# Soft-capped attention and a maxout layer on one core: three buffers for q and k, with their loads and crossbar transposes moved forward in the order

## The chip, the cores and the metric

The kernel runs on one core of a Trainium2 chip. Its time is the device time of one execution in microseconds (us); lower is better. Several runs were timed, and one more execution was taken by the hardware profiler, which is where all instruction times below come from.

The engines by the profile's names: PE is the matrix engine (PEld its weight loads), DVE the vector engine, ACT the scalar engine with its function tables, POOL the GpSimd engine, which here issues loads, and SP the sync engine, which here issues crossbar transposes and stores. A "q" behind an engine's name is its instruction queue.

## What is computed

Attention over 8 batches of 12 heads, 448 rows and 64 columns, with a soft cap of 30 on the scores; then a layer that takes the larger of two products, and an output product. The reference, cut:

```python
scores = scale * np.matmul(q, k.transpose(0, 1, 3, 2))     # (8, 12, 448, 64) each
scores = cap * np.tanh(scores / cap)
scores = scores - np.max(scores, axis=-1, keepdims=True)
attn = np.exp(scores)
attn = attn / (np.sum(attn, axis=-1, keepdims=True) + 1e-09)
attn_out = np.matmul(attn, v)
...
x = attn_out.transpose(0, 2, 1, 3).reshape(B * S, H * D)   # 3584 x 768
h1 = x @ w1                                                # 768 x 1024
h2 = x @ w2
g = np.maximum(h1, h2)
return g @ w_out                                           # 1024 x 768
```

## The kernel before

**Tiling.** Two heads of one batch make a pair, two pairs a quad. There are 48 pairs and 24 quads, three quads to a batch. The maxout layer is rewritten: max(h1, h2) = h2 + max(h1 - h2, 0), so the kernel prepares w1 - w2 (`wd_sb`) and w2 times w_out (`wm_sb`) once, and the layer needs a product with `wd_sb` (stage 1), a relu (L619), and products with `wm_sb` and `wo_sb` (stage 2).

**The order.** Nothing is left to a scheduler. The string `ORDER` (from L9) lists some 2300 steps, and the loop at L699 runs them one after the other; each step emits a few instructions, and every engine and queue executes its own in this order. Where an instruction needs a buffer or data of another engine, it waits there, and what is behind it on the same engine waits too. A step's place in `ORDER` relative to steps on other engines has no force of its own: it matters only through the waits, and through what stands before it on its own engine.

**The steps that matter here.**

- `lk i x`, `lq i 0` (`load`, L318): POOL issues loads of k and q of pair i into `kqs`, turning f32 into bf16 on the way. From pair 10 on (`NX = 10`) k comes in two parts and q in one (L329), so a quad has four k loads and two q loads. A quad's rows lie in `kqs[t % KB]`, with `KB = 2` buffers (L267, L270).
- `cr t` (`cross`, L443): from quad 5 on SP issues one crossbar transpose (a DMA) that turns the whole quad from `kqs` into a `qkT` buffer, of which there are `QB = 2` (L415, L445). In the first five quads PE does this turning with an identity matrix (L430), and DVE copies the result (L435).
- `S i j` (`scores`, L473): PE multiplies k and q of pair i from `qkT` (L478), for row block j of three. `L t` (L485, L491) does the left-over 64 rows of both pairs of quad t. A score tile is one of two `s` buffers in PSUM.
- `T`, `TL`, `E`, `EL`: ACT's tanh (L483, L495) and exponential (L499, L502).
- `A`, `B`, `Y`, `Y1` to `Y3`: sums of the exponentials and their inverses, on DVE and PE.
- `lv t p` (`load_v`, L331): POOL issues the four loads of the values of quad t, with `VB = 2` buffers, so that they wait for the values product of quad t-2.
- `V t u` (`values`, L553): PE multiplies the exponentials with the values (L561, L565), and `N` (L574) scales the result on DVE into `xT`. `V t` comes after the scores of pair 2t + 2, so some one and a half quads after the scores of quad t begin.
- `M x y n` (`moe`, L677): n matmuls each of groups x and y of the layer (L598), put between the attention's steps to fill PE. `H` is a hand-over between the two halves of a group, `ev` copies a finished group out of PSUM (L619 for stage 1, L652 for stage 2 into one of four `osb` buffers).
- `st b t` (`store`, L623): SP issues the two stores of an output tile (L634, or L629 and L630).

So in the steady state four chains meet: POOL's loads fill `kqs`, SP turns `kqs` into `qkT`, PE reads `qkT`, and the buffers go back: loads of quad t wait until the transpose of quad t - KB has landed, and the transpose of quad t waits until its loads have landed and until PE has read the last scores of quad t - QB, which are `S 2(t-QB)+1 2`.

Two queues carry the moved steps. On POOL the `lk`, `lq` and `lv` steps stand in one line; on SP the `cr` and `st` steps do. In the old order, quad 11 (pairs 22 and 23) as an example, POOL has

```
lk 22 0; lk 22 1; lq 22 0; lk 23 0; lk 23 1; lv 9 0..3; lq 23 0; lk 24 0; ...
```

and SP has `cr 7; st 0 0; st 0 1; cr 8; st 0 2; cr 9; st 1 3; cr 10; st 1 4; st 1 5; cr 11; st 1 6; cr 12`.

Of the kernel before, what the change touches and what calls it, by code (L numbers as in the profile page):

```python
# [14 lines left out]
WC 0; T 1 1; OP 0 0 0; P 0 0 2; T 1 2; P 0 0 1; S 2 0; lk 4 0; P 0 0 1; P 1 0 1; E 1 0 2; P 1 0 1; lw1 0;
S 2 1; P 1 0 2; P 2 0 1; lwo 1 0; P 2 0 1; PC 1 0; P 2 0 2; T 2 0; P 0 0 1; lk 5 0; PC 2 0; X 3 3; lw2 3;
E 1 2 3; P 0 0 1; XC 3; S 2 2; lwo 1 1; P 0 0 2; T 2 1; PC 0 0; lq 5 0; T 2 2; X 4 2; lq 6 0; L 1; lv 1 0;
XC 4; Y 0 1; TL 1; lv 1 1; sub 0 0; V 0 0; E 2 0 3; V 0 1; Y1 0; S 3 0; Y2 0; Y3 0; lv 1 2; OP 0 1 3; P 0 1 1;
T 3 0; N 0 0; P 0 1 3; lv 1 3; N 0 1; OP 2 1 0; P 2 1 2; EL 1; P 2 1 2; S 3 1; S 3 2; T 3 1; OP 1 1 2; P 1 1 2;
# [185 lines left out]
def kernel(  # L205
# [17 lines left out]
    B, H, S, D = q.shape  # L223
# [15 lines left out]
    WOP = 2  # L239
    R7 = S // 64  # L240
# [495 lines left out]
```

## Time and profile before

| | |
|---|---|
| runs | 340.12, 339.49 and 338.31 us; median 339.49 |
| profiled execution: span | 339.5 us |
| PE busy, matmuls | 327.9 us (97%), 4076 |
| PEld busy | 194.0 us (57%) |
| DVE busy | 229.4 us (68%) |
| ACT busy | 275.3 us (81%) |
| POOL busy | 169.9 us (50%) |
| chain that ended last | PE 79%, DMA 7%, DVE 6%, ACT 5% |
| q and k loads, issue to landing (median) | 5.5 us (q), 4.1 us (k) |
| values loads `vp`, issue to landing (median) | 5.7 us |
| crossbar transposes | 19; issue to landing 4.2 to 13.8 us, median 7.1 |
| stores, issue to landing (median) | 4.8 us |

The profile has a page with sums, and the trace behind it can be asked for the waits, for a timeline and for sums over a stretch of time. Busy time on PE is made of modelled ends of matmuls, so that a short stop can hide in it; starts are measured. A wait's releaser is inferred from semaphore events. Idle time of an engine that others don't wait for costs nothing.

### The profile page before, as it was taken

The numbers are of one execution on the slowest core, as the hardware profiler recorded it, in microseconds if no ns is written. First come the engines' busy times: TensorE is split into PE (matmuls) and PEld (weight loads), VectorE is DVE, ScalarE is ACT, GpSimd is POOL, SyncE is SP. The second block draws the span as 40 slices with busy tenths as digits, with TensorE's granted clock in tenths as the row PEclk, the third lists the DMA queues.
The fourth block names the chain that finished last, engine by engine and source line by source line (L and its number), as shares of the span: only waits on it lengthen the run. The fifth ranks groups of instructions, "written<-read, shape, count | busy, mean of one in ns | idle before, by whom it ended". The sixth has DMA issues, their size and how long they took to land.

```text
span 339.5 us, 9672 instructions
## 1 busy us (share of the span) xinstructions
PE 327.9 (97%) x4076; PEld 194.0 (57%) x4076; DVE 229.4 (68%) x411; ACT 275.3 (81%) x267; POOL 169.9 (50%) x250
## 2 busy tenths in 40 slices
PE   8999999999999999899999999999999999999994
PEld 5644556555767555555655564656565555567662
DVE  2355789786796659667788568856976778774321
ACT  2899989999989998888999998899899999810000
POOL 7476779766674562591871663658737302000000
PEclk9999999999999999999999999999999999999998
DMA  8999999999999999999998999999999963013033
GB/s 144 189 172 188 250 216 99 131 134 183 150 143 129 143 141 113 146 118 132 207 138 84 133 156 190 122 102 220 184 114 126 193 137 48 2 47 95 2 95 93
DMA packets 136108, 45.90 MB, mean 135 GB/s; under 512 B 116352, under 2 KB 131072, under 8 KB 136064
## 3 DMA queue, kind: packets, MB, share of 16 engines
q0 software_dynamic: 96320, 25.08, 76.4%
q1 hardware_dynamic: 39440, 19.86, 33.6%
q8 instruction: 32, 0.52, 0.6%
q10 hardware_dynamic: 304, 0.33, 0.3%
q14 instruction: 12, 0.10, 0.1%
HBM read 47.45 MB, written 11.01 MB: 172 GB/s over the span
## 4 chain that ended last, share of the span: by engine, by line
PE 79%; DMA 7%; DVE 6%; ACT 5%; issue 1%; DVEq 0%
PE mm L598 50%; PE s L478 8%; DMA qkT<-kqs 7%; PE s L561 5%; PE mm L403 4%; ACT e L499 3%; PE mm L441 2%; PE s L491 2%; PE s L565 2%; PE mm L536 2%; PE mm L430 1%; ACT e L483 1%; DVE xT L574 1%; PE mm L388 1%; DVE esum L511 1%
## 5 line engine op out<-in xcount | busy, mean ns | idle before, releaser
L483 ACT ACTIVATE e<-s 128x896 bf16<-128x896 f32 x144 | 127.7, 929 | 6.7 <-PE s L478 6.6
L499 ACT ACTIVATE e<-e 128x2688 bf16<-128x2688 bf16 (+2 forms) x72 | 122.8, 1707 | 0.0
L598 PE MATMUL mm<-wo_sb,gT 64*128 64x384 bf16 x864 | 114.5, 323 | 0.0
L598 PE MATMUL mm<-wm_sb,xT 64*128 64x384 bf16 x648 | 101.0, 323 | 0.0
L598 PE MATMUL mm<-xT,wd_sb 64*128 64x448 bf16 x768 | 99.1, 349 | 0.6 <-DVE gT L619 0.4
L329 POOL DMA_DIRECT2D kqs<-in_k_dram x76 | 54.2, 716 | 71.5 <-DMA qkT<-kqs 71.3
L598 PEld LDWEIGHTS <-gT 64*128 64x128 bf16 x864 | 59.2, 94 | 25.1 <-DVEq L607 0.2
L598 PEld LDWEIGHTS <-wd_sb 64*128 64x128 bf16 x768 | 52.1, 94 | 24.7 <-issue 2.6
L598 PEld LDWEIGHTS <-xT 64*128 64x128 bf16 x648 | 50.4, 94 | 18.6 <-issue 0.6
L478 PE MATMUL s<-qkT 64*128 64x448 bf16 x288 | 56.0, 358 | 3.6 <-DMA qkT<-kqs 1.9
L619 DVE TENSOR_SCALAR gT<-mm 128x448 bf16<-128x448 f32 x64 | 39.6, 622 | 15.0 <-PE mm L598 14.6
L652 DVE COPY osb<-mm 128x384 f32<-128x384 f32 x54 | 29.4, 555 | 25.2 <-PE mm L598 19.8
L511 DVE TENSOR_TENSOR esum<-e 128x896 bf16<-128x896 bf16 x42 | 26.1, 621 | 23.1 <-ACT e L499 16.0
L347 POOL DMA_DIRECT2D vp<-in_v_dram x48 | 30.4, 638 | 22.5 <-PE mm L598 11.1
L329 POOL DMA_DIRECT2D kqs<-in_q_dram x38 | 35.3, 930 | 4.1 <-DMA kqs<-in_k_dram 1.8
L561 PE MATMUL s<-e,vp 128*32 128x448 bf16 x576 | 35.8, 352 | 0.0
L478 PEld LDWEIGHTS <-qkT 64*128 64x128 bf16 x288 | 16.6, 94 | 29.2 <-issue 13.5
L495 ACT ACTIVATE el<-s 128x896 bf16<-128x896 f32 x24 | 22.0, 917 | 13.9 <-PE s L491 13.3
L347 POOL DMA_DIRECT2D vl<-in_v_dram x48 | 29.3, 618 | 6.8 <-DMA wo_sb<-in_moe_w_out_dram 4.1
L662 ACT COPY osb<-mm 128x192 f32<-128x192 f32 x1 | 0.3, 320 | 36.8 <-DMA out_dram<-osb 36.8
L574 DVE TENSOR_TENSOR xT<-s,inv 128x448 bf16<-128x448 f32 x48 | 27.7, 620 | 3.0 <-PE mm L598 0.5
L511 DVE TENSOR_TENSOR esum<-esum,e 128x896 bf16<-128x896 bf16 x42 | 26.2, 624 | 2.2 <-PE mm L598 0.4
(56 smaller groups left out, 272.0 us busy)
## 6 DMA issues: line engine op xcount, KB each, us to landing
out_dram<-osb SPq DMA_DIRECT2D x54, 192.0 KB, 4.8
vp<-in_v_dram POOLq DMA_DIRECT2D x38, 160.0 KB, 5.7
kqs<-in_q_dram POOLq DMA_DIRECT2D x47, 112.0 KB, 5.5
kqs<-in_k_dram POOLq DMA_DIRECT2D x76, 56.0 KB, 4.1
osb<-in_moe_w_dram POOLq DMA_DIRECT2D x4, 512.0 KB, 7.1
gT<-in_moe_w_dram POOLq DMA_DIRECT2D x6, 256.0 KB, 5.9
wo_sb<-in_moe_w_out_dram POOLq DMA_DIRECT2D x4, 384.0 KB, 8.8
xT<-in_moe_w_dram POOLq DMA_DIRECT2D x2, 512.0 KB, 6.7
```

The lines of the kernel that those rows point to most:

```text
L329: nc.gpsimd.dma_start(out=to, in_=x)
L347: nc.gpsimd.dma_start(out=to, in_=x)
L478: nc.tensor.matmul(s[:, h, :S], k_of(t, o, h, j), q_of(t, o, h))
L483: nc.scalar.activation(expo[i][:, 2 * j : 2 * j + 2, :], slots[i, j][:, :, :S], AF.Tanh, scale=scale / cap)
L495: nc.scalar.activation(left_e[t], slots[t][:, :, :S], AF.Tanh, scale=scale / cap)
L499: nc.scalar.activation(e, e, AF.Exp, scale=float(cap))
L511: nc.vector.tensor_add(d, e[:, 0:2, :] if j == 1 else d, e[:, 2 * j : 2 * j + 2, :])
L561: nc.tensor.matmul(ps[r, u, :S], vp[t % VB][:, m, j if turned_by_pe(t) else 2 * j, u::2], expo[2 * t + o][:, 2 * j + h, :], start=(j == 0) ...
L574: nc.vector.tensor_mul(x, vals[t][:, u, :S], sums[t, 3])
L598: ins = nc.tensor.matmul(self.ps, w[r], x[r], start=first, stop=self.at == [self.n, self.n]).ins
L619: nc.vector.tensor_relu(gT[b // 2][:, f, cs], ps)
L652: nc.vector.tensor_copy(o[:, hs], ps)
```

## The change

`KB` and `QB` go from 2 to 3, which adds one buffer for a quad's loaded rows and one for its turned rows. In `ORDER` nothing is added or removed, and all other steps keep their order: 119 of the `lk`, `lq` and `cr` steps stand further forward. The loads of pairs 14 and 15 (quad 7) move some 20 steps, those of pairs 16 and 17 some 45, those of 18 and 19 some 60 to 65, and from pair 20 on 80 to 95 steps; a quad is some 84 steps in the steady state. `cr 7` moves 17 steps, `cr 8` 38, `cr 9` 51, the later ones 64 to 72. `cr 5` and `cr 6` stay.

```diff
-M 5 4 1; ev 3; M 5 4 1; EL 4; M 5 4 1; lv 5 3; S 9 2; A 4 0 1; O 6 3; M 6 4 2; lk 13 1; M 6 4 1; T 9 1; H 5;
...
-ev 10; M 13 12 3; lk 18 0; A 5 1 2; T 12 2; M 13 12 3; ev 11; M 13 12 1; lk 18 1; L 6; Y 5 3; TL 6; V 5 0;
...
-T 29 1; M 56 54 1; M 56 55 1; cr 16; M 56 55 1; H 54 2; M 56 55 1; M 54 55 1; T 29 2; M 54 55 1; H 56; S 30 0;
...
-L 15; lk 36 0; Y 14 3; TL 15; V 14 0; Y1 14; lk 36 1; V 14 1; E 30 0 3; Y2 14; lq 36 0; Y3 14; S 31 0;
...
+O 5 1; M 5 3 2; T 9 0; H 4; M 5 3 1; ev 2; lv 5 2; S 9 1; M 5 4 1; ev 3; M 5 4 1; lk 14 0; EL 4; M 5 4 1; lv 5 3;
+S 9 2; A 4 0 1; O 6 3; M 6 4 2; lk 14 1; lk 13 1; M 6 4 1; T 9 1; H 5; A 4 0 2; M 6 5 3; lq 14 0; lq 13 0; ev 4;
...
+Y3 4; S 11 0; M 10 9 1; lv 6 0; lk 17 0; N 4 0; M 10 9 2; M 8 9 1; N 4 1; M 8 9 1; lk 18 0; lk 17 1; lv 6 1; M 8 9 2;
...
+S 28 0; H 52; M 53 51 2; M 53 52 1; E 27 0 2; M 53 52 1; ev 51; S 28 1; M 53 52 7; T 28 0; M 53 52 1; cr 16; A 13 1 1;
...
+M 54 53 1; M 52 53 1; T 28 1; M 52 53 2; A 13 1 2; M 52 53 2; M 52 53 1; T 28 2; M 52 53 2; L 14; lk 36 0; ev 52;
...
-    KB = 2
+    KB = 3
     VB = 2
-    QB = 2
+    QB = 3
```

On POOL the loads of quad 7 now stand between those of quad 6: `lk 13 0; lv 5 0; lv 5 1; lv 5 2; lk 14 0; lv 5 3; lk 14 1; lk 13 1; lq 14 0; lq 13 0; lk 15 0; ...`, where the old order has `lk 13 0; lv 5 0..3; lk 13 1; lq 13 0; lk 14 0; lk 14 1; lq 14 0; lk 15 0; ...`. A little later it reads `lv 6 0; lk 17 0; lk 18 0; lk 17 1; lv 6 1; lv 6 2; lk 18 1; lq 17 0; lv 6 3; lq 18 0; ...`, and from there on `lv t` stands ahead of the loads of quad t+3 or t+4 instead of t+2 or t+3. On SP the new order begins `cr 7; st 0 0; cr 8; st 0 1; st 0 2; cr 9; cr 10; st 1 3; cr 11; st 1 4; st 1 5; cr 12; st 1 6; cr 13`.

More of the change, by code (lines that the diff above doesn't have):

```diff
@@ L15 @@
[L15 to L19, printed above, removed]
@@ new lines @@
+P 3 1 4; lw2 5; P 0 1 3; T 4 0; P 0 1 1; P 1 1 1; lv 2 0; P 1 1 1; PC 0 1; P 1 1 2; E 3 2 3; P 2 1 1; lv 2 1; PC 1 1;
+S 4 2; X 5 3; lv 2 2; T 4 1; P 2 1 1; XC 5; P 2 1 1; lv 2 3; P 2 1 1; T 4 2; OP 3 0 2; P 3 0 2; PC 2 1; lw1 4; L 2;
+Y 1 3; lk 6 0; TL 2; V 1 0; lk 7 0; Y1 1; E 4 0 3; V 1 1; Y2 1; Y3 1; S 5 0; lq 7 0; N 1 0; W 5 0; lw1 2; W 4 3;
+N 1 1; T 5 0; P 3 0 1; WC 5; P 3 0 1; lw1 5; S 5 1; EL 2; P 3 0 1; lw1 1; WC 4; S 5 2; P 3 0 1; lq 8 0; T 5 1;
+P 3 0 2; P 3 1 2; PC 3 0; P 3 1 1; T 5 2; lk 8 0; P 3 1 1; OP 4 0 0; P 4 0 1; sub 4 0; P 4 0 3; lk 9 0; E 5 0 2;
@@ new lines @@
+X 6 3; PC 3 1; lq 9 0; P 4 0 2; XC 6; P 4 0 2; lw1 3; X 7 2; PC 4 0; S 6 0; XC 7; S 6 1; T 6 0; OP 5 0 1; P 5 0 2;
+lv 3 0; sub 2 0; P 5 0 3; E 5 2 3; P 5 0 1; S 6 2; P 5 0 2; T 6 1; OP 4 1 3; P 4 1 1; lv 3 1; sub 5 0; P 4 1 4; T 6 2;
+P 4 1 2; L 3; PC 5 0; Y 2 0; lv 3 2; TL 3; V 2 0; sub 1 1; Y1 2; E 6 0 3; V 2 1; Y2 2; Y3 2; S 7 0; N 2 0; X 8 2;
+lv 3 3; N 2 1; X 9 1; T 7 0; lq 10 0; XC 8; P 4 1 1; EL 3; S 7 1; XC 9; S 7 2; lq 11 0; OP 5 1 0; P 5 1 2; PC 4 1;
+P 5 1 1; T 7 1; P 5 1 1; A 3 0 1; P 5 1 2; lk 10 0; P 5 1 2; T 7 2; sub 3 0; O 0 2; M 0 -1 1; lk 10 1; S 8 0;
@@ new lines @@
+M 12 10 1; lk 19 1; M 12 10 1; M 12 11 2; H 10 2; M 12 11 1; M 10 11 2; H 12; lq 19 0; M 10 11 1; T 12 0; A 5 1 1;
+M 10 11 2; M 10 11 2; B 5 0; M 10 11 1; E 11 2 3; O 13 1; M 13 11 1; S 12 2; M 13 11 1; B 5 1; M 13 11 1; M 13 12 1;
+T 12 1; M 13 12 1; ev 10; lk 20 0; M 13 12 3; A 5 1 2; T 12 2; M 13 12 3; ev 11; M 13 12 1; lk 20 1; L 6; Y 5 3;
+lq 20 0; TL 6; V 5 0; cr 8; Y1 5; st 0 1; V 5 1; lk 21 0; E 12 0 3; Y2 5; Y3 5; S 13 0; M 13 12 1; lk 21 1; lv 7 0;
+N 5 0; M 13 12 1; O 14 0; M 14 12 2; H 13; N 5 1; lv 7 1; M 14 12 1; M 14 13 2; H 12 2; S 13 1; lv 7 2; T 13 0;
@@ new lines @@
+A 6 0 1; M 14 13 1; M 12 13 2; lv 7 3; M 12 13 1; H 14; A 6 0 2; EL 6; M 12 13 1; S 13 2; M 12 13 1; M 12 13 2;
+T 13 1; M 12 13 1; O 15 3; M 15 13 1; lq 21 0; M 15 13 1; ev 12; M 15 13 1; M 15 14 1; T 13 2; M 15 14 1; ev 13;
+S 14 0; M 15 14 1; O 16 2; M 16 14 1; E 13 0 2; M 16 14 1; H 15; S 14 1; M 16 14 1; st 0 2; M 16 15 2; ev 14;
+M 16 15 1; O 17 1; M 17 15 2; H 16; T 14 0; M 17 15 1; A 6 1 1; M 17 16 3; ev 15; O 18 0; M 18 16 1; E 13 2 3; S 14 2;
+M 18 16 1; H 17; B 6 0; M 18 16 1; M 18 17 1; T 14 1; M 18 17 1; ev 16; M 18 17 1; O 19 3; M 19 17 2; lk 22 0; B 6 1;
@@ new lines @@
+T 14 2; M 19 17 1; H 18; cr 9; ev 17; M 19 18 3; A 6 1 2; O 20 2; M 20 18 1; lk 22 1; M 20 18 2; L 7; ev 18; Y 6 1;
+TL 7; lq 22 0; V 6 0; Y1 6; V 6 1; E 14 0 3; Y2 6; lk 23 0; Y3 6; S 15 0; M 20 19 1; lk 23 1; N 6 0; M 20 19 1;
+lv 8 0; M 20 19 1; N 6 1; O 21 0; M 21 19 2; lv 8 1; M 21 19 1; H 20; S 15 1; T 15 0; ev 19; M 21 20 1; lv 8 2;
+M 21 20 2; A 7 0 1; O 22 1; M 22 20 1; EL 7; M 22 20 1; lv 8 3; S 15 2; H 21; A 7 0 2; M 22 20 1; M 22 21 1;
+M 22 21 1; T 15 1; ev 20; lq 23 0; M 22 21 1; O 23 3; M 23 21 1; M 23 21 1; H 22; M 23 21 1; T 15 2; M 23 22 1;
@@ new lines @@
+S 17 1; M 25 24 2; lv 9 2; O 26 3; M 26 24 1; A 8 0 2; EL 8; M 26 24 1; S 17 2; M 26 24 1; lv 9 3; H 25; M 26 25 2;
+T 17 1; H 24 2; M 26 25 1; lk 25 1; M 24 25 1; M 24 25 1; H 26; M 24 25 2; T 17 2; M 24 25 1; lq 25 0; S 18 0;
+M 24 25 2; E 17 0 2; M 24 25 1; S 18 1; O 27 1; M 27 25 1; ev 24; M 27 25 2; M 27 26 2; ev 25; M 27 26 3; T 18 0;
+cr 11; M 27 26 1; A 8 1 1; M 27 26 3; st 1 4; M 27 26 1; B 8 0; E 17 2 3; M 27 26 1; S 18 2; O 28 2; M 28 26 1; H 27;
+B 8 1; M 28 26 2; T 18 1; M 28 27 2; H 26 2; A 8 1 2; M 28 27 1; M 26 27 2; T 18 2; M 26 27 2; lk 26 0; L 9; Y 8 0;
@@ new lines @@
+S 26 0; M 45 44 1; ev 43; M 45 44 1; E 25 0 2; M 45 44 1; S 26 1; O 46 1; M 46 44 1; H 45; M 46 44 2; st 2 2;
+M 46 45 2; ev 44; M 46 45 1; O 47 0; M 47 45 1; T 26 0; A 12 1 1; M 47 45 2; H 46; ev 45; E 25 2 3; cr 15; M 47 46 1;
+S 26 2; M 47 46 1; B 12 0; M 47 46 1; O 48 3; M 48 46 1; T 26 1; M 48 46 1; H 47; B 12 1; M 48 46 1; M 48 47 1;
+M 48 47 1; ev 46; T 26 2; M 48 47 1; lk 34 0; O 49 2; M 49 47 2; H 48; A 12 1 2; M 49 47 1; lk 34 1; M 49 48 2; ev 47;
+M 49 48 1; L 13; Y 12 1; lq 34 0; TL 13; V 12 0; Y1 12; V 12 1; lk 35 0; E 26 0 3; Y2 12; Y3 12; S 27 0; lk 35 1;
@@ new lines @@
+M 54 55 1; H 56; S 30 0; M 54 55 3; E 29 0 2; M 54 55 1; S 30 1; cr 17; M 54 55 2; O 57 2; M 57 55 2; ev 54;
+M 57 55 1; M 57 56 2; ev 55; M 57 56 1; T 30 0; M 57 56 2; A 14 1 1; M 57 56 3; E 29 2 3; M 57 56 1; st 3 4; B 14 0;
+S 30 2; lk 38 0; M 57 56 2; B 14 1; O 58 0; M 58 56 1; T 30 1; M 58 56 2; H 57; A 14 1 2; lk 38 1; M 58 57 2; T 30 2;
+M 58 57 1; H 56 2; M 56 57 1; L 15; lq 38 0; Y 14 3; TL 15; V 14 0; Y1 14; V 14 1; lk 39 0; E 30 0 3; Y2 14; Y3 14;
+lk 39 1; S 31 0; M 56 57 1; N 14 0; M 56 57 1; lv 16 0; M 56 57 2; N 14 1; M 56 57 2; lv 16 1; M 56 57 1; O 59 3;
@@ new lines @@
+O 63 3; M 63 61 1; M 63 61 1; lk 40 1; H 62; M 63 61 1; ev 60; st 3 6; lq 40 0; L 16; ev 61; M 63 62 1; TL 16; Y 15 1;
+lk 41 0; V 15 0; Y1 15; E 32 0 3; lk 41 1; V 15 1; Y2 15; lq 41 0; Y3 15; S 33 0; M 63 62 1; lv 17 0; N 15 0;
+M 63 62 1; O 64 2; M 64 62 1; N 15 1; M 64 62 1; lv 17 1; M 64 62 1; T 33 0; H 63; ev 62; S 33 1; lv 17 2; M 64 63 2;
+A 16 0 1; M 64 63 1; EL 16; lv 17 3; O 65 1; M 65 63 1; S 33 2; H 64; A 16 0 2; M 65 63 2; T 33 1; M 65 64 2; ev 63;
+M 65 64 1; O 66 0; M 66 64 1; T 33 2; M 66 64 1; H 65; S 34 0; M 66 64 1; M 66 65 2; E 33 0 2; ev 64; S 34 1;
@@ new lines @@
+M 66 65 1; O 67 3; M 67 65 2; H 66; M 67 65 1; M 67 66 2; ev 65; M 67 66 1; cr 19; T 34 0; O 68 2; M 68 66 1;
+A 16 1 1; M 68 66 2; E 33 2 3; H 67; ev 66; M 68 67 1; S 34 2; M 68 67 1; B 16 0; M 68 67 1; T 34 1; lk 42 0; O 69 1;
+M 69 67 2; H 68; B 16 1; M 69 67 1; M 69 68 1; lk 42 1; M 69 68 1; T 34 2; ev 67; M 69 68 3; M 69 68 1; A 16 1 2;
+M 69 68 4; lq 42 0; L 17; Y 16 0; TL 17; V 16 0; Y1 16; lk 43 0; V 16 1; E 34 0 3; Y2 16; Y3 16; S 35 0; lk 43 1;
+M 69 68 1; N 16 0; O 70 3; M 70 68 3; H 69; N 16 1; M 70 69 2; lv 18 0; M 70 69 1; H 68 2; S 35 1; T 35 0; H 70;
@@ new lines @@
+A 17 0 1; M 68 69 1; lv 18 1; M 68 69 3; A 17 0 2; M 68 69 1; EL 17; lv 18 2; M 68 69 1; S 35 2; M 68 69 2; lq 43 0;
+lv 18 3; O 71 0; M 71 69 1; T 35 1; M 71 69 1; ev 68; M 71 69 1; M 71 70 2; ev 69; T 35 2; M 71 70 1; S 36 0;
+M 71 70 3; E 35 0 2; M 71 70 1; S 36 1; st 4 0; M 71 70 4; O 72 2; M 72 70 2; H 71; cr 20; M 72 70 1; M 72 71 1;
+T 36 0; M 72 71 1; A 17 1 1; M 72 71 1; H 70 2; H 72; B 17 0; M 70 71 1; E 35 2 3; M 70 71 1; S 36 2; M 70 71 1;
+B 17 1; M 70 71 1; M 70 71 1; T 36 1; M 70 71 2; A 17 1 2; M 70 71 1; lk 44 0; O 73 1; M 73 71 1; T 36 2; M 73 71 1;
@@ new lines @@
+M 80 79 1; S 39 2; lv 20 2; A 19 0 1; O 81 1; M 81 79 3; T 39 1; H 80; lq 47 0; lv 20 3; A 19 0 2; M 81 80 1;
+M 81 80 2; ev 79; O 82 0; M 82 80 1; T 39 2; M 82 80 1; S 40 0; H 81; M 82 80 1; M 82 81 1; E 39 0 2; M 82 81 1;
+ev 80; S 40 1; M 82 81 1; O 83 3; M 83 81 2; H 82; cr 22; M 83 81 1; M 83 82 2; ev 81; M 83 82 1; T 40 0; M 83 82 2;
+A 19 1 1; M 83 82 2; E 39 2 3; M 83 82 1; S 40 2; B 19 0; M 83 82 3; B 19 1; T 40 1; O 84 2; M 84 82 2; M 84 82 1;
+H 83; A 19 1 2; M 84 83 2; T 40 2; M 84 83 1; H 82 2; M 82 83 1; L 20; Y 19 1; TL 20; V 19 0; Y1 19; V 19 1; E 40 0 3;
@@ new lines @@
+M 87 86 3; T 42 1; B 20 1; M 87 86 3; ev 85; M 87 86 1; T 42 2; M 87 86 2; A 20 1 2; O 88 2; M 88 86 3; H 87; st 5 4;
+M 88 87 1; L 21; Y 20 1; TL 21; V 20 0; Y1 20; V 20 1; E 42 0 3; Y2 20; Y3 20; S 43 0; M 88 87 1; lv 22 0; N 20 0;
+M 88 87 1; M 86 87 2; H 88; N 20 1; M 86 87 1; lv 22 1; M 86 87 3; S 43 1; lv 22 2; T 43 0; A 21 0 1; M 86 87 2;
+O 89 1; M 89 87 1; lv 22 3; M 89 87 1; ev 86; EL 21; M 89 87 1; S 43 2; M 89 88 1; A 21 0 2; M 89 88 2; T 43 1;
+M 89 88 1; ev 87; M 89 88 1; M 89 88 3; T 43 2; M 89 88 1; S 44 0; M 89 88 1; st 5 5; M 89 88 1; O 90 0; M 90 88 1;
@@ new lines @@
+E 43 0 2; M 90 88 1; H 89; S 44 1; M 90 88 1; M 90 89 2; H 88 2; M 90 89 1; M 88 89 2; H 90; M 88 89 1; T 44 0;
+M 88 89 1; A 21 1 1; M 88 89 3; B 21 0; M 88 89 1; E 43 2 3; O 91 3; M 91 89 1; S 44 2; B 21 1; M 91 89 2; T 44 1;
+M 91 90 1; ev 88; M 91 90 2; A 21 1 2; T 44 2; O 92 2; M 92 90 3; H 91; ev 89; L 22; ev 90; M 92 91 1; TL 22; Y 21 1;
+V 21 0; st 5 6; Y1 21; E 44 0 3; V 21 1; Y2 21; Y3 21; S 45 0; M 92 91 1; lv 23 0; N 21 0; M 92 91 1; O 93 0;
+M 93 91 1; N 21 1; M 93 91 1; lv 23 1; M 93 91 1; T 45 0; H 92; ev 91; S 45 1; lv 23 2; M 93 92 2; A 22 0 1;
@@ L201 @@
+M 116 114 1; M 116 115 2; H 114 2; M 116 115 1; M 114 115 2; H 116; M 114 115 6; O 117 2; M 117 115 2; ev 114;
+M 117 115 1; M 117 116 2; ev 115; M 117 116 7; st 7 4; M 117 116 2; M -1 116 2; H 117; M -1 116 1; M -1 117 2;
+H 116 2; M -1 117 1; M 116 117 8; M -1 117 2; ev 116; M -1 117 1; O 118 1; M 118 118 1; ev 117; M 118 118 7; st 7 5;
+M 118 118 6; O 119 0; M 119 119 2; ev 118; M 119 119 12; ev 119; st 7 6;
 """
```

282 lines of the change are left out of this document (100 added, 182 removed).

## The prediction

> **What bounds the kernel now.** I read first how busy each engine is in stretches of 10 us, to find where the busiest one stops. The columns are the stretch, then busy microseconds of PE, PEld, DVE, ACT and POOL with their numbers of instructions, the granted clock, the DMA share and GB/s.
>
> ```profile
> 120.00:130.00 10.00, 9.88 (x124) 6.15 (x113) 6.83 (x14) 10.00 (x11) 7.17 (x10) 1.00 1.13 130
> 130.00:140.00 10.00, 8.20 (x100) 3.70 (x101) 7.37 (x14) 8.97 (x9) 0.44 (x1) 1.00 1.23 121
> 140.00:150.00 10.00, 9.25 (x124) 5.70 (x120) 8.12 (x14) 7.71 (x8) 9.62 (x14) 1.00 1.39 139
> 220.00:230.00 10.00, 9.37 (x118) 5.08 (x116) 6.53 (x13) 9.55 (x11) 5.43 (x8) 1.00 1.42 108
> 60.00:270.00 210.00, 206.40 (x2594) 122.30 (x2594) 156.93 (x279) 197.72 (x191) 125.21 (x177) 1.00 1.37 146
> ```
>
> PE works through one fixed list and is busy 206.4 of the 210 us that the change touches; the clock is 1.00 throughout. So the time is PE's work plus its idle time, and all that loads can give back there is 3.6 us. 3.2 us of that (1.80, 0.75, 0.63) lies in three stretches. Next, who waits for whom, longest first (total, times, longest), and the timeline around 139 us, with the idle time before a row in brackets:
>
> ```profile
> POOL kqs L329 <- DMA qkT<-kqs: 71.3, 12, 10.5
> PE s L478 <- DMA qkT<-kqs: 1.9, 2, 1.5
> SPq L445 <- DMA kqs<-in_q_dram: 76.9, 16, 10.2
> ...
> 125.21 3.96 SPq L445 DMA_TRANSPOSE qkT<-kqs  x1
> 136.07 1.49 PE L598 MATMUL mm<-xT,wd_sb 64*128 64x448 bf16 x14
> 139.08 0.36 PE L478 MATMUL s<-qkT 64*128 64x448 bf16 x2 [1.52 <-DMA qkT<-kqs]
> 139.56 1.40 POOL L329 DMA_DIRECT2D kqs<-in_k_dram  x2 [10.47 <-DMA qkT<-kqs]
> 149.46 0.36 PE L478 MATMUL s<-qkT 64*128 64x448 bf16 x2 [0.75 <-ACT e L483]
> ```
>
> Here is the loop of two buffers. POOL may load quad t+2 only when the crossbar transpose of quad t has landed (71.3 us of waiting), and SP may issue the transpose only when those loads have landed (76.9 us). In quad 11 the transpose is issued at 125.21 and takes 13.8 us to land (the chain of waits has it as one piece of 13.82); the scores of pair 22 (S 22 0) wait for it. The other case is quad 18: issued at 214.73, 9.3 us, S 36 0 at 224.08 after 0.41 us of idle. The other transposes arrive before PE asks, so the 71.3 and 76.9 us cost nothing by themselves.
>
> **The change, part by part.**
>
> *Taken away: the two late transposes.* PE's ends are modelled, so I count by starts. The 14 matmuls at 136.07 run in 7 pairs; their last pair starts 0.35 us before their end, at 137.21, and pairs follow each other by 1.14/6 = 0.19 us, so S 22 0 could have started at 137.40: 139.08 - 137.40 = 1.7 us. In the same way at 224.08 (six matmuls from 223.02 to 223.67, pairs 0.16 apart): 0.6 us. With three buffers the transpose of quad t waits for the last scores of quad t-3. For quad 11 these are S 17 2, at 112.06; even with the worst landing seen, 13.8 us, it is there at 126.3, 11 us before 137.4. So both waits go: -2.3 us. What comes next on PE there is the list itself.
>
> *The gap at 149.46.* PE waits 0.75 us for ACT ten microseconds behind the first stall. If that is its echo it goes (0.9 us by starts), if ACT is late of itself it stays. I can't tell from the rows, and take the middle, -0.4, with ends 0 and -0.9.
>
> *Moved: the loads.* Each still costs POOL 0.71 us (k) or 0.92 us (q) to issue, and as many are issued; POOL is 60% busy in 60 to 270 us. From lk 16 on they move by about half a quad to a quad, past the four value loads (lv) of one quad; nothing on POOL is on PE's path while values have slack (rivals). But at the start of the new order three loads of quad 7 come ahead of lk 13 1 and lq 13, the last of quad 6:
>
> ```profile
> 62.09 1.27 POOL L347 DMA_DIRECT2D vp<-in_v_dram  x2 [2.06 <-PE s L565]
> 63.33 1.23 POOL L347 DMA_DIRECT2D vl<-in_v_dram  x2
> 64.52 0.75 POOL L329 DMA_DIRECT2D kqs<-in_k_dram  x1
> 65.26 0.92 POOL L329 DMA_DIRECT2D kqs<-in_q_dram  x1
> 66.18 1.41 POOL L329 DMA_DIRECT2D kqs<-in_k_dram  x2
> 67.58 0.92 POOL L329 DMA_DIRECT2D kqs<-in_q_dram  x1
> ...
> 69.00 9.22 SPq L445 DMA_TRANSPOSE qkT<-kqs  x2
> 77.76 0.35 PE L478 MATMUL s<-qkT 64*128 64x448 bf16 x2
> ```
>
> The row at 65.26 is lq 13; it lands 3.5 us later, at 68.8, and cr 6 goes out at 69.00 and lands 6.8 us later, at 75.8; S 12 0 wants it at 77.76, 2.0 us of slack. Now lk 14 0, lk 14 1 and lq 14 (1.41 + 0.92 = 2.3 us, the rows at 66.18 and 67.58) stand before it, and all of them stand behind lv 5, which can't start before 62.0 since it waits for PE's values of quad 3 (L565). So cr 6 lands at 78.1 and PE waits 0.3 to 0.4 us. The three transposes nearest to it (issued at 56.84, 69.00 and 76.50) took 6.6 to 6.8 us, all beside k and q loads alone, as this one will be: lv 6 is held behind lk 18 0, which waits for cr 6 itself. Cost +0.4, ends 0 (a landing in the 4.2 us of the last one) and +2 (a landing in 8.8 us, as at 112.45). Queued behind that wait of POOL are lk 17 1, lq 17 and lv 6 1 to 3; lv 6 is wanted at 96.2 and quad 8 at 102, so 15 us and more are left.
>
> *Moved: the transposes on SP.* As many, 1.5 to 4.0 us each to issue. They pass stores: st 0 1 is now behind cr 8, st 1 3 behind cr 10, st 3 4 behind cr 17, and so on. A store is held while a transpose waits for its loads, and loads are now issued more than a quad ahead of it, so I expect shorter holds. Where stores were held before, DVE waited for an output buffer twice (2.62 us before 189.15, 2.08 us before 236.45), and PE for DVE's copies 0.2 us twice. Value taken 0, ends -0.4 and +0.4.
>
> *The first five quads* also get three buffers, but their order stays. PE waits for no load there; POOL's first loads wait 0.7 us for PE's scores in all. Value 0, ends -0.5 and 0.
>
> Sum against the profiled 339.5 us, which is the median of the runs shown (339.49): -1.7 - 0.6 - 0.4 + 0.4 = -2.3, so **337.2 us**, 0.7% less.
>
> **The rivals.**
>
> *Values come late (slower).* Loads, transposes and stores share the 16 DMA engines, whose mean share is 1.37 in 60 to 270 us: something waits in them most of the time. The new order asks for a whole quad more of q and k by the time of V 7 and V 8: four k and two q loads, 4 x 0.71 + 2 x 0.92 = 4.7 us, and a transpose of 6.6 us, so 11 us of traffic that wasn't before them. Loads that are issued in the same time as a transpose are held by it: those of 65 to 66 us land after 3.1 to 3.5 us, lv 10, issued at 125.0 to 126.9 beside the transpose of 125.21, lands after 8.0 to 11.4 us. Value loads can't go earlier, since with VB = 2 they wait for V t-2, and in the new order their gate opens some 3 us before the transpose's, quad after quad. lv 10 lands at about 137.8 and V 10 starts at 145.43: 7.6 us of slack. If all 11 us fall on the values and the idle moments of the queues don't take them up, V 10 is 3.4 us late, and a slack of the same size is missed at two or three more quads: 337.2 + 3.4 to 337.2 + 9, some 341 to 346 us. It decides from about 8 us of lasting delay. For it speaks the long landing times of value loads; against it, that each quad's traffic is the same and only its first extra quad is new, and that POOL's 71 us of waiting, which also holds value loads (those of quad 10 were issued at 125.01 though V 8 was done at 120.8), goes. Chance 0.15.
>
> The Trainium skill speaks for this rival: DMA: Bandwidth & Descriptors, Queues, rings and completion order, says that each DMA engine serves its queue rows in turn, packet by packet. By that rule a transpose with loads always beside it is always a slow one, as at 125.21, and none of the gain is safe; the trace agrees in part, since the landings run from 4.2 to 13.8 us.
>
> *The stall goes elsewhere (no change).* ACT is busy 197.7 of 210 us in the same stretch, 94%, so PE has little to run ahead into: the two stalls shrink but the gap at 149.46 stays or grows, and cr 6 costs its upper end of 2 us: 339.5 - 2.3 + 2 = 339.2, or 338.3 with half of it. For it: ACT's chain of 2.44 us exponentials ends just before 149.46. Against: ACT itself waits 6.6 us for scores. Chance 0.25.
>
> *More than the stalls (faster).* All of the 3.2 us in the three stretches goes, and the store waits too (0.4), with nothing lost at cr 6: 335.9, or 335.4 with the first quads' half microsecond. Chance 0.1.
>
> **How the numbers follow.** The forecast has 0.5, with a range of its own from 336.2 to 338.3 (echo at either end, cr 6 between 0 and 1). A change of under 0.5%, 1.7 us, can't be told from none here. Faster than 337.8: 0.40 of the forecast's 0.5 and the 0.1 of the last rival, 0.5. Slower than 341.2: 0.13 of the first rival. Between: the rest, 0.37. The range, 335.6 to 341.0, takes in the no-change rival whole and leaves out most of the slower one and the tip of the faster.
>
> **What would show it.** Right: no PE wait of over 0.3 us for qkT after 100 us; a small one (0.3 to 0.5 us) at S 12 0 near 77.8 us; POOL's 71.3 us of waiting for qkT falls below 30 us and waits for V (L565) take its place; the transposes land 10 us and more before their scores. Wrong: weight loads or matmuls of L561 or L565 that wait for vp or vl, which is the slower rival; a gap for ACT at the first S of odd pairs, which is the no-change one.

## The result: slower by half a per cent to one per cent, and the profile after

The changed kernel took 342.47, 345.01, 341.52 and 343.53 us, median 343.0; the kernel before, with one more run, has a median of 339.81. The ratio is 1.0106, with a 95% interval from 1.0072 to 1.0139. Two later sessions gave 1.0080 (1.0048 to 1.0113) and 1.0045 (1.0014 to 1.0076). The ratios leave out executions that are more than 1.5% above the fastest of their kernel; of the changed kernel that takes out some that are slow by its own doing (the clock, below), so its ratios are rather low.

First the stretches of 10 us of the changed kernel, in the columns used before.

```profile
70.00:80.00 10.00, 8.80 (x120) 4.68 (x116) 7.09 (x13) 9.39 (x10) 5.60 (x8) 1.00 1.57 145
130.00:140.00 10.00, 9.59 (x119) 5.08 (x115) 9.17 (x17) 8.96 (x10) 5.17 (x8) 1.00 1.52 162
...
60.00:270.00 210.00, 206.51 (x2594) 122.22 (x2592) 156.83 (x279) 197.10 (x191) 124.97 (x174) 1.00 1.32 145
```

From 130 to 140 us PE is busy 9.59 us instead of 8.20: the late transpose of quad 11 is gone. But PE's idle time from 60 to 270 us is 3.5 us, as before (3.6). More than half of it, 1.9 us, now stands just before 80.70 us. The waits say for what (total, times, longest):

```profile
POOL vp L335 <- PE s L553: 71.3, 16, 8.8
...
POOL kqs L317 <- DMA qkT<-kqs: 8.5, 3, 5.2
...
PE s L466 <- DMA qkT<-kqs: 1.9, 1, 1.9
```

The loop of two buffers is broken: POOL waits 8.5 us for transposes, not 71.3, and its waiting has moved to the values (L553, the line that was L565). PE has one wait for `qkT` left, of 1.9 us. The timeline shows where it comes from:

```profile
64.83 0.77 POOL L317 DMA_DIRECT2D kqs<-in_k_dram  x1
65.59 0.62 POOL L335 DMA_DIRECT2D vl<-in_v_dram  x1
66.20 1.47 POOL L317 DMA_DIRECT2D kqs<-in_k_dram  x2
67.67 1.85 POOL L317 DMA_DIRECT2D kqs<-in_q_dram  x2
69.52 1.44 POOL L317 DMA_DIRECT2D kqs<-in_k_dram  x2
70.95 0.93 POOL L317 DMA_DIRECT2D kqs<-in_q_dram  x1
71.88 1.44 POOL L317 DMA_DIRECT2D kqs<-in_k_dram  x2
73.31 0.93 POOL L317 DMA_DIRECT2D kqs<-in_q_dram  x1
...
74.28 4.64 SPq L433 DMA_TRANSPOSE qkT<-kqs  x2
...
78.31 0.49 PE L586 MATMUL mm<-wo_sb,gT 64*128 64x384 bf16 x4
80.70 0.36 PE L466 MATMUL s<-qkT 64*128 64x448 bf16 x2 [1.90 <-DMA qkT<-kqs]
...
150.73 0.37 PE L466 MATMUL s<-qkT 64*128 64x448 bf16 x2 [0.75 <-ACT e L471]
```

The second q load of the row at 67.67 is `lq 13`, issued at 68.60. It lands at 74.16, 5.6 us later, with `lq 14` ahead of it landed at 71.11. `cr 6` goes out at 74.28 and lands at 80.66, 6.4 us later, and `S 12 0` starts at 80.70. Set against the profile of before, step by step, PE's starts shift by +0.6 us near 52 us, by **+2.1 at `S 12 0`**, by -1.7 at `S 22 0`, by -0.6 at `S 36 0`, and by little else. The last row is the gap of 0.75 us for ACT, still there.

### The profile page after: what moved, and what is told of

Same layout as the page of the kernel before. It is cut to its first block, busy times and chain, and to the rows that moved or that the text cites. A ratio compares the mean times of both kernels' runs of the same rounds, so it can differ in the third digit from the quotient of the medians.

```text
span 340.6 us, 9655 instructions
## 1 busy us (share of the span) xinstructions
PE 328.1 (96%) x4076; PEld 194.2 (57%) x4076; DVE 231.3 (68%) x411; ACT 275.2 (81%) x267; POOL 170.5 (50%) x250
## 4 chain that ended last, share of the span: by engine, by line
PE 77%; DVE 9%; ACT 7%; issue 3%; DMA 2%; DVEq 0%
PE mm L586 50%; PE s L466 8%; PE s L549 6%; ACT e L487 4%; PE mm L391 3%; PE mm L429 2%; PE s L479 2%; DVE wd_sb L365 2%; ACT e L471 2%; DMA qkT<-kqs 2%; PE s L553 2%; PE mm L524 2%; DVE esum L504 1%; PE mm L418 1%; DVE xT L562 1%
## 5 line engine op out<-in xcount | busy, mean ns | idle before, releaser
L335 POOL DMA_DIRECT2D vp<-in_v_dram x48 | 30.4, 636 | 85.3 <-PE s L553 71.3
```

The source lines that it names most:

```text
L335: nc.gpsimd.dma_start(out=to, in_=x)
```

## The experiments

PE's loss at a step is the growth, there, of its starts' distance to those of the first profile of before. A median stands beside that of the kernel before in the same session.

**The kernel before again, and third buffers alone.** The first is unchanged; the second is the kernel before with its own order and

```diff
-    KB = 2
+    KB = 3
-    QB = 2
+    QB = 3
```

> The kernel before once more, for a second profile and more times. Theory A (the two late transposes of the profile before are a matter of chance, and that execution was a slow one of its kernel): ratio 1.000, and in this profile the waits of PE for qkT at S 22 0 and S 36 0 are smaller or sit at other quads, with a span nearer 338 than 339.5 us. Theory B (they are part of every execution): the same two waits, 1.7 and 0.6 us by starts, and a span of 339.5 us.

> Three buffers each, but the old order. POOL still runs ahead of its place in the order wherever a buffer is free. Theory A (what costs is the place of quad 7's loads ahead of quad 6's last ones, and a collision of DVE and POOL near 46 us): no wait at S 12 0, no wait at S 22 0 and S 36 0, the collision's 0.6 us stays; ratio 0.996 to 1.002. Rival (the extra quad of traffic costs as such): slower than before by about as much as the change, ratio 1.008 to 1.012, with waits for qkT, vp or vl.

Measured: 339.43 us against 339.20, ratio 1.0010 (0.9993 to 1.0026), and 339.92 us, ratio 1.0020 (1.0005 to 1.0035). What matters is the new profile of the kernel before, first its stretches, then its timeline:

```profile
130.00:140.00 10.00, 9.60 (x118) 4.70 (x115) 8.40 (x16) 8.96 (x9) 5.44 (x9) 1.00 1.31 128
...
60.00:270.00 210.00, 208.43 (x2618) 123.58 (x2616) 158.53 (x282) 199.23 (x194) 126.06 (x178) 1.00 1.36 147
```

```profile
136.89 1.49 PE L598 MATMUL mm<-xT,wd_sb 64*128 64x448 bf16 x14
138.22 0.35 PE L478 MATMUL s<-qkT 64*128 64x448 bf16 x2
...
148.59 0.37 PE L478 MATMUL s<-qkT 64*128 64x448 bf16 x2 [0.75 <-ACT e L483]
```

The scores of `S 22 0`, here at 138.22, follow the 14 matmuls without a wait, and so do those of quad 18: quad 11's transpose took 8.0 us and landed 4.2 us early. PE is idle for 1.6 us of the 210, and half of that is the gap for ACT. In all 14 other profiles of this document PE's starts gain 1.7 us at `S 22 0` and 0.6 us at `S 36 0` on those of the first; two of them have two buffers, this one and the old order with three loads ahead, below. So the two stalls on which the forecast stood belong to one execution, not to the kernel; third buffers, which end their cause, gain nothing in the median.

**Quad 6's last loads first.** The changed kernel with POOL's steps in this order:

```diff
-lk 14 0; lv 5 3; lk 14 1; lk 13 1; lq 14 0; lq 13 0
+lk 13 1; lq 13 0; lk 14 0; lv 5 3; lk 14 1; lq 14 0
```

and a second kernel that has two buffers in the first five quads besides.

> The changed kernel with one edit: lk 13 1 and lq 13 0 stand ahead of lk 14 0 again. Theory A: S 12 0 no longer waits (2.1 us by the shift of the two traces), all else as in the changed kernel; 2.1 us less than the changed kernel, ratio to before 1.003 to 1.006. Rival (the extra traffic): the wait goes to a later quad or to the values, and the ratio stays at 1.010.

> As the one before, and the first five quads keep two of the three buffers for their rows, so that POOL's loads of the start wait as they did. Theory A: POOL's and DVE's subtractions near 46 us meet as in the kernel before, DVE's takes 1.2 us and not 3.1, and another 0.6 us goes: ratio 1.000 to 1.004. Rival (the collision is chance and not the buffers): it still appears or appears in either, and the ratio is that of the kernel without this edit.

Measured: 339.46 us, ratio 1.0017 (1.0002 to 1.0031), and 339.25, ratio 1.0001 (0.9982 to 1.0021), with no wait for `qkT` in either profile. Two steps of `ORDER` carry the loss; the other moves, nearly all of the change, gain nothing and cost at most the 0.3% at which the first interval ends.

**The changed kernel again; two loads ahead; early buffers.** The second kernel here moves `lq 13` up by one place, the third gives the first five quads two buffers.

```diff
-lk 14 1; lk 13 1; lq 14 0; lq 13 0; lk 15 0
+lk 14 1; lk 13 1; lq 13 0; lq 14 0; lk 15 0
...
+    def ring(t):
+        return t % 2 if t < NX // 2 else t % KB
...
-kqs[t % KB]
+kqs[ring(t)]
```

> The changed kernel again, beside the kernel before in the same session. Theory A (the three loads of quad 7 ahead of the last two of quad 6 hold the transpose of quad 6, and S 12 0 waits for it in every execution): S 12 0 waits 1.5 to 2.5 us again, ratio to before 1.006 to 1.010, that is 341.2 to 342.6 against 339.2. Theory B (the long landing of lq 13, 5.56 us instead of 3.5, was chance of the profiled execution, and the slow times one session's): S 12 0 waits 0 to 0.5 us, ratio 0.998 to 1.003. The collision of the two subtracts near 46 us: if it is set by the order it comes again (VectorE's subtract over 3 us, +0.5 us), if chance it takes about 1.2 us.

> The changed kernel with lq 13 one place sooner: only lk 14 0 and lk 14 1 are ahead of quad 6's last loads, lq 14 behind them. The issue of lq 13 comes 0.93 us sooner, at about 67.7. Theory A1 (a fixed stretch near 71 to 74 us in which nothing lands; what is issued before it escapes): lq 13 lands at about 71.1, cr 6 at 77.6, no wait at S 12 0, ratio 1.000 to 1.003. Theory A2 (lq 13's landing is long by its place among loads, 5.6 us from its issue): cr 6 lands at about 79.7, S 12 0 waits about 1.2 us, ratio 1.003 to 1.007.

> The changed kernel, but the first five quads use two buffers. Theory A: as the changed kernel, 1.5 to 2.5 us at S 12 0, ratio 1.005 to 1.010. If third buffers in the first quads set the collision of VectorE's and GpSimd's subtracts near 46 us, this is 0.5 us faster than the changed kernel and its VectorE subtract takes 1.2 us; if the collision is chance, no difference in the median beyond 0.3 us.

Measured, before at 339.59: 342.17 us, ratio 1.0080 (1.0048 to 1.0113); 339.66, ratio 1.0016 (0.9995 to 1.0038); 340.64, ratio 1.0034 (1.0010 to 1.0058). In the two-ahead kernel `lq 13` landed at 70.76 and `cr 6` at 77.99, just in time. One place further back, the load lands 3 us later, not 0.9: in this profile and in those of the changed kernel there is a stretch of 3 us, ending between 73 and 75 us, in which no load lands, and then three land within 0.6 us. In the two-ahead kernel `lq 14` is caught in it instead, harmlessly. That speaks for theory A1 and against A2; the kernel with five loads ahead, below, fits neither.

In the changed kernel's new profile the wait is longer, and something else follows it, first in the timeline, then in stretches of 1 us (the granted clock is the third column from the right):

```profile
80.98 0.36 PE L466 MATMUL s<-qkT 64*128 64x448 bf16 x2 [3.15 <-DMA qkT<-kqs]
```

```profile
81.00:82.00 1.00, 1.00 (x10) 0.56 (x12) 0.00 (x0) 0.62 (x1) 0.53 (x1) 0.72 1.28 296
82.00:83.00 1.00, 1.00 (x10) 0.45 (x8) 0.00 (x0) 1.00 (x2) 1.00 (x3) 0.50 0.94 252
83.00:84.00 1.00, 1.00 (x10) 0.50 (x8) 0.00 (x0) 0.94 (x2) 1.00 (x2) 0.50 1.13 96
84.00:85.00 1.00, 1.00 (x11) 0.44 (x7) 0.48 (x1) 0.00 (x0) 1.00 (x3) 0.57 1.22 90
85.00:86.00 1.00, 1.00 (x16) 0.61 (x14) 0.95 (x3) 0.00 (x0) 1.00 (x2) 1.00 1.19 143
```

After 3.15 us of idleness PE runs at half clock: ten matmuls in a microsecond, where the last row, at full clock, has 16. The four rows below 1.00 lack 0.28 + 0.50 + 0.50 + 0.43 = 1.7 us of full clock, so it lasted some 3.4 us, and PE's starts show the same 1.7 us (0.4 by `S 12 1`, 1.3 by `S 12 2`). By starts the wait is 3.3 us, so the loss is 3.3 + 1.7 = 5.0 us.

**The three loads ahead in the old order.** The kernel before, two buffers, with

```diff
-lk 13 1; lq 13 0; lk 14 0; lk 14 1; lq 14 0
+lk 14 0; lk 14 1; lq 14 0; lk 13 1; lq 13 0
```

> The kernel before with its two buffers and its order, but lk 14 0, lk 14 1 and lq 14 put ahead of lk 13 1 and lq 13. Theory A (their place alone costs, without third buffers and without the later moves): S 12 0 waits 0.5 to 2.5 us, ratio 1.002 to 1.009; with a landing of lq 13 as in the changed kernel (5.6 us) the upper half of it, with one of 3.5 us the lower. Theory C (it takes the longer run of loads behind it, quad 8's too, to hold lq 13 and the transpose): no wait at S 12 0, ratio 0.999 to 1.002.

Measured: 339.69 us against 339.59, ratio 1.0000 (0.9977 to 1.0024). `lq 13` is late (72.32), `cr 6` is issued at 72.44, but it lands in 4.0 us, and PE's weight loads wait 0.2 us. So theory A, that the place alone costs, is wrong. With two buffers POOL can't load quad 8 before `cr 6` has landed, so beside the transpose there are only quad 7's last three loads and the four of `lv 6`, which POOL issues from 74.12 us on.

**Quad 8's loads held, and five loads ahead.** The first is the changed order with two buffers up to quad 8, so that `lk 16` waits for `cr 6`:

```diff
+    def ring(t):
+        return t % 2 if t < 9 else (t + 1) % KB
...
-kqs[t % KB]
+kqs[ring(t)]
```

In this kernel quad 9's keys go into quad 7's buffer ahead of its transpose: quad 7's scores are computed with them, and `cr 7` waits for `lk 18`. The second has `lk 15 0; lk 15 1` ahead of `lq 13` too.

> The changed kernel with its order, but quads 5 to 8 use two buffers in turn, so that lk 16 and lq 16 (quad 8) wait until the transpose of quad 6 has landed: beside it only lk 15 and lq 15 still run. lq 13 stays behind the three loads of quad 7. Theory A (lq 13 comes late, whatever runs beside the transpose): cr 6 is issued at about 74 and lands after 6.3 to 7.3 us, S 12 0 waits 1.5 to 2.5 us, ratio to before 1.006 to 1.010. Theory C (the late lq 13 is half of it, the loads of quad 8 beside the transpose the other half; with them held the transpose lands in about 4 us, as in the kernel before with the three loads ahead, 4.04 us): cr 6 lands at about 78.3, S 12 0 waits 0 to 0.5 us, ratio 0.999 to 1.003.

> The changed kernel with lq 13 two places later: lk 15 0 and lk 15 1 are ahead of it as well, its issue comes 1.44 us later, at about 70.0. Theory A1 (nothing lands between about 71 and 74 us, whatever was issued last): lq 13 lands at 74.1 to 74.8, at the end of that stretch, S 12 0 waits 0.2 to 0.7 us more than in the changed kernel (2.1 to 3.2), ratio 1.007 to 1.011. Theory A2 (the landing is so many us from the issue, 5.5): lq 13 lands at about 75.5, S 12 0 waits 1.4 us more (3.5 to 4.6). If PE's wait is above 3 us, the granted clock falls to 0.5 behind it, as in the repeated profile of the changed kernel, and costs 1.5 us more: ratio 1.012 to 1.018.

Measured: the first, 342.92 us against 339.27, ratio 1.0082 (1.0051 to 1.0113). At `S 12 0` theory C came out: `cr 6` landed in 3.4 us and PE lost nothing there. But the late `cr 7` cost 2.9 us at `S 14 0`, so its time decides nothing. The second, 342.28 us, ratio 1.0078 (1.0052 to 1.0103): `lq 13` was issued at 69.11, 1.5 us later than in the changed kernel's second profile, and landed at 72.95, 0.6 us sooner, and sooner than either theory had it; the loss at `S 12 0` was 1.7 us. Further loads ahead cost nothing more.

**Quad 8's loads held, mended.** From quad 9 on the buffers go round the other way, so that quad 9's keys no longer go into quad 7's buffer. Beside it the changed kernel and its early-buffer variant once more.

```diff
-        return t % 2 if t < 9 else (t + 1) % KB
+        return t % 2 if t < 9 else 2 - t % KB
```

> As the run before it with quad 8's loads held, but from the tenth quad on the buffers go round the other way, so that quad 9's keys don't take quad 7's buffer ahead of its transpose. Theory C: cr 6 is issued at about 74 and lands in 3.4 to 4.5 us, S 12 0 waits 0 to 0.5 us; cr 7 follows it within some 2 us, so that S 14 0 doesn't wait either; ratio 0.999 to 1.003, that is 339.0 to 340.3 against 339.3. Theory A: S 12 0 waits 1.5 to 2.5 us, ratio 1.006 to 1.010.

> The changed kernel a third time, beside the next one. If its time is the wait at S 12 0 (2 to 3 us) and now and then a spell of half clock behind it: ratio 1.006 to 1.010 and a wait of 1.5 to 3.5 us in the profile; the clock below 0.995 in the runs that take 2 us more than the others.

> The changed kernel with two buffers in the first five quads, again beside the changed kernel. If these buffers matter: ratio 1.001 to 1.006 and 1 to 2 us less than the changed kernel in the same session. If they don't (the wait at S 12 0 is the same 2 us): the two lie within 0.5 us of each other, ratio 1.005 to 1.010.

Measured, before at 339.13: **338.68 us**, ratio 0.9987 (0.9969 to 1.0006); the changed kernel 341.25, ratio 1.0045 (1.0014 to 1.0076); with two buffers in the first quads 342.36, ratio 1.0024 (0.9992 to 1.0055). The timeline of the held kernel (the row at 72.62 is `cr 6` and `cr 7`), then its stretch from 60 to 270 us. The last two rows are of the loads' queue, between the issue of `cr 6` and its landing (packets, MB, share of the engines' time), for the changed kernel's third profile and for the held kernel:

```profile
72.62 3.33 SPq L436 DMA_TRANSPOSE qkT<-kqs  x2
...
77.13 0.49 PE L589 MATMUL mm<-wo_sb,gT 64*128 64x384 bf16 x4
77.45 0.35 PE L469 MATMUL s<-qkT 64*128 64x448 bf16 x2
```

```profile
60.00:270.00 210.00, 208.41 (x2622) 124.16 (x2616) 157.84 (x280) 199.74 (x194) 126.99 (x178) 1.00 1.36 149
```

```profile
q0 software_dynamic: 2226, 0.41, 86.4%
...
q0 software_dynamic: 579, 0.07, 30.5%
```

`lq 13` is still behind three loads of quad 7 and lands at 72.50, but `cr 6` takes 3.7 us and `S 12 0` at 77.45 doesn't wait. What is held is `lk 16 0` and, behind it on POOL, the four loads that in the changed kernel still run beside `cr 6` (`lk 16 1`, `lq 16`, `lv 6 0`, `lk 17 0`). That gives back all of the loss, in the median 2.6 us. It isn't the two buffers in the first quads, which the held kernel has too: the early-buffer variant has them without the hold, and in the same session its profile lost 5.2 us at `S 12`. Nor is it that `cr 7` now goes out while `cr 6` is in flight, 1.9 us behind it in the changed kernel's first profile: in the held kernel it is 1.7 us behind. What the early buffers are worth by themselves stays open: 1.5 us below the changed kernel in one session, 1.1 above it in the next, with its ratio below the changed kernel's both times and the intervals overlapping.

All the numbers of quad 6 together (us; "beside" tells whether quad 8's loads run beside `cr 6`, and how many MB the loads' queue moved in all between its issue and its landing):

| kernel | loads of quad 7 ahead of `lq 13` | `lq 13` issued, landed | beside | `cr 6` issued, took | PE's loss by `S 12 2` |
|---|---|---|---|---|---|
| before, 1st profile | 0 | 65.26, 68.79 | no, 0.42 | 69.00, 6.8 | 0 |
| before, again | 0 | 66.10, 69.43 | no, 0.44 | 69.63, 7.3 | 0 |
| third buffers alone | 0 | 64.58, 68.31 | no, 0.47 | 68.50, 7.2 | 0 |
| quad 6 first | 0 | 64.23, 68.33 | yes, 0.44 | 68.51, 7.9 | 0 |
| quad 6 first, early two | 0 | 64.01, 68.11 | yes, 0.42 | 68.36, 6.9 | 0 |
| two ahead | 2 | 67.24, 70.76 | yes, 0.51 | 70.84, 7.2 | 0 |
| changed, 1st profile | 3 | 68.60, 74.16 | yes, 0.42 | 74.28, 6.4 | 2.1 |
| changed, 2nd | 3 | 67.63, 73.52 | yes, 0.38 | 73.64, 7.3 | 5.0 |
| changed, 3rd | 3 | 67.92, 73.37 | yes, 0.41 | 73.49, 5.8 | 1.3 |
| early two, 1st | 3 | 69.88, 75.40 | yes, 0.41 | 75.52, 6.3 | 2.0 |
| early two, 2nd | 3 | 67.79, 73.53 | yes, 0.40 | 73.66, 7.7 | 5.2 |
| five ahead | 5 | 69.11, 72.95 | yes, 0.48 | 73.07, 6.3 | 1.7 |
| old order, three ahead | 3 | 67.96, 72.32 | no, 0.18 | 72.44, 4.0 | 0 |
| quad 8 held | 3 | 69.10, 74.78 | no, 0.01 | 74.90, 3.4 | 0 |
| quad 8 held, mended | 3 | 67.84, 72.50 | no, 0.07 | 72.62, 3.7 | 0 |

Where `cr 6` goes out by 71 us, it has time for 7 to 9 us before PE asks. After 72 us it has time for 4 to 6, and takes that little only without quad 8's loads. The loss needs both halves. What `cr 6` takes goes with what the loads move beside it: 3.4 to 4.0 us with 0.01 to 0.18 MB, 5.8 to 7.9 with 0.38 to 0.51; early in the program it is quad 7's loads that run beside it.

## Why the prediction was wrong, point by point

**The baseline** is the first step that failed: "Sum against the profiled 339.5 us, which is the median of the runs shown (339.49)". The 339.5 us is a span, and the time of an execution is some 1.8 us more: 342.47 for a span of 340.6, 339.78 for 338.0. So the profiled execution took about 341.3 us, an estimate, 1.8 above the median, and the 2.3 us of its two late transposes account for that. The second profile hasn't got them, nor has any later one.

**"Taken away: the two late transposes", -2.3.** As a comparison of two profiles it is exact, -1.7 and -0.6, and in the changed kernel's profiles the transposes from quad 7 on land 9 to 20 us before their scores, much as foreseen. Against the median it is 0.

**"The gap at 149.46", -0.4.** It isn't an echo: a gap of 0.74 or 0.75 us stands there in all 15 profiles, with the stall ahead of it or without. The value is 0, one of the ends.

**"Moved: the loads", +0.4.** The place, the steps and the wait were right, the size was not: 2.1, 5.0 and 1.3 us in three profiles. The mis-sized term is `lq 13`'s landing, taken as 3.5 us after its issue, because the row before had it; it took 5.5 to 5.9. That gave `cr 6` a start at 71.3 by the sum, and 73.5 to 74.3 in the profiles. Its 6.8 us was nearly right (5.8 to 7.3), but the reason given was not: value loads (`lv 4`, `lv 6`) were in flight beside all three transposes that were read as "beside k and q loads alone", and `lv 6 0` stands ahead of `lk 18 0`, not behind it; it went out at 74.63, beside `cr 6`. That third buffers let quad 8's loads run there too, and that they set what `cr 6` takes, was not asked. And the half clock behind a long wait was not in the sum at all. (The ends of the forecast's own range add up to 336.3 and 338.2, not 336.2 and 338.3; nothing hangs on it.)

The sum with these numbers: the kernel before has a median of 339.2 us over its 110 runs in the four sessions. With 2.1 us it is 341.3. Of the changed kernel's 23 executions, 16 have a mean granted clock of 0.995 or more and a median of 341.3 us; the 7 with 0.988 to 0.993 have a median of 345.0.

**"Transposes past stores" and "the first five quads", 0.** The first is borne out by the kernels with quad 6 first and with quad 8 held, which keep these moves and lie within 0.2% of before. The second isn't contradicted.

**The rivals.** Values didn't come late: their loads now land 3.7 us after issue in the median, 5.7 before. The Trainium skill's rule that was cited for that rival (DMA: Bandwidth & Descriptors, Queues, rings and completion order: an engine serves its queue rows in turn) agrees with another pair of rows: `cr 6` took 3.4 to 4.0 us behind the late `lq 13` without quad 8's loads, 5.8 to 7.7 with them. It hit quad 6's transpose, not the values. "The stall goes elsewhere" had the right ingredients, the gap that stays and `cr 6` at its upper end, but its 339.2 counted the 2.3 us as won.

## What to carry to other kernels

Before a stall of one profile is counted as a gain, add to the span what lies around it and set that against the median; where the profiled execution is slower than the median, its stalls may be what makes it so, and a second profile tells. When loads are moved forward, look first at the place where the new order begins: the last load that the next transpose needs must not stand behind loads of a later one, and loads that a new buffer sets free will run beside that transpose. If the engine that bounds the kernel idles for 3 us, count the clock that it loses as well.

## What the runs showed of the hardware

**The clock falls after about 3 us.** PE waits of 1.15, 1.57, 1.79, 1.90 and 2.58 us, counted from the modelled ends of matmuls, left the granted clock at 1.00; 3.15 and 3.38 us took it to 0.50 for some 3.4 us. The Trainium skill (TensorE: Matmul & The Clock Gate, What's actually happening) has half the clock after one idle window of about 3.4 us, of a grid that runs freely; the half agrees, and here 3.15 us, by modelled ends, were enough.

**Where two subtractions meet, one takes longer.** DVE and POOL share out the preparation of `wd_sb`. In the changed kernel's first profile they overlapped, in its second they did not; rows of both engines, the first profile, then the second:

```profile
46.18 2.15 POOL L365 TENSOR_TENSOR wd_sb<-osb,gT 128x1024 bf16<-128x1024 f32 x1
...
46.26 3.15 DVE L365 TENSOR_TENSOR wd_sb<-xT,gT 128x1024 bf16<-128x1024 f32 x1
```

```profile
45.85 1.22 DVE L365 TENSOR_TENSOR wd_sb<-xT,gT 128x1024 bf16<-128x1024 f32 x1
...
47.54 2.15 POOL L365 TENSOR_TENSOR wd_sb<-osb,gT 128x1024 bf16<-128x1024 f32 x1
```

It took DVE 3.15 us instead of 1.22, POOL 2.15 us in both, and PE lost some 0.6 us near 52 us. DVE's subtraction is drawn out like that in 3 of 15 profiles (3.15, 3.28 and 3.69 us), with two and with three buffers in the first quads; in other profiles of the changed kernel and of its early-buffer variant it is not, so it goes with the execution and not with the kernel. In both profiles of before the two overlap for only 0.4 to 0.5 us: there DVE takes 1.22 us, and POOL 2.46 and 2.39. Which of them gives way is not settled here. The Trainium skill (GPSIMD Engine Reference, Specifications) says that GpSimd shares its SBUF interfaces with VectorE and contends with instructions of two SBUF inputs, as these are.

**A stretch without landings is not one without transfers.** Between about 70 and 74 us no load lands for 3 us in the changed kernel's profiles, but the DMA engines are fuller there than on the average. In the second profile, the last two columns being the DMA share and GB/s:

```profile
70.20:73.50 3.30, 3.30 (x58) 1.60 (x54) 2.43 (x5) 2.69 (x4) 3.09 (x4) 1.00 1.77 116
```

The share is 1.77 against the 1.36 to 1.37 of the stretch from 60 to 270 us in the kernel before, and nothing but loads and one packet of instructions moves. Between the issue of `lq 13` and its landing the loads' queue moves 0.58 MB; `lq 13` has 112 KB, the four loads in flight ahead of it 240 KB together, so at least 0.2 MB belongs to loads that were issued after it. So the loads aren't stopped: they share the engines, and several land together. Why `lq 13` gets so little of them at this place stays open, and with it why its landing comes 2 us later than the sum had it.
